# The second experts' transposed rows share the first layer's PSUM buffers

## Chip, cores and metric

The kernel runs on one core of a Trainium2 chip. The metric is the time of one execution on the device in microseconds (us). The engines of the core work side by side and wait for each other by semaphores: TensorE (PE in the rows; PEld is its weight load) multiplies matrices into PSUM, VectorE (DVE), ScalarE (ACT) and GpSimd (POOL) do the rest of the arithmetic, SyncE (SP) and GpSimd start transfers (DMAs).

## What is computed

Three layers follow each other: an attention with a local window and block summaries, a mixture of experts in which every row picks its best expert, and a second mixture in which each of eight experts takes exactly 384 rows, in the order of the scores. The third is where the change lies:

```python
def _moe2_ref(x, w_gate, w1, w2):
    N, D = x.shape            # 3072, 512
    E = w_gate.shape[1]       # 8
    cap = N // E              # 384
    logits = x @ w_gate
    order = np.argsort(-logits.flatten())
    ...                       # each row to its best expert that still has room
    for e in range(E):
        mask = assigned == e
        h = np.maximum(x[mask] @ w1[e], 0.0)      # 384 x 1024
        out[mask] = h @ w2[e]                     # 384 x 512
    return out
```

## The kernel before

The program runs in phases: attention (from the start to about 300 us), the first experts, and `phase_d`, the second experts, from about 340 us on. In `phase_d` three kinds of work are woven together on the engines. What is woven is fixed when the program is built: a small scheduler at the end of `phase_d` keeps estimated clocks (`now`, `dve`, `pool`) and decides in which order the pieces are written; at run time each engine goes through its own list in order and waits on semaphores.

The experts. One expert at a time has its 384 rows multiplied. Its first layer, `L1`, makes eight sums `dh_ps` (128 columns of the hidden layer each), each of 12 products (lines 961, 962, 963: high rows by high weights, low rows by high weights, high rows by low weights; four depth blocks). ScalarE (line 966) and VectorE (line 968) read each sum. Its second layer, `L2`, makes three sums `dz_ps` of 24 products (lines 975, 976, 977). A step counter `npc` runs over the 32 steps of the first layer and the 24 of the second.

The rows of the next expert. GpSimd gathers them (line 939, three gathers of 128 rows, tile `xg`) once the list of rows is ready; TensorE transposes each gather's 128 rows in four blocks into PSUM (line 950, `xT`); ScalarE copies them out as the high part `dxh` and VectorE subtracts to make the low part `dxl` (both on line 953). The scheduler puts the three groups of transposes (groups 0, 1 and 2 below) into the second layer of the expert before, at steps 34, 38 and 42 or later (`xts_step`). For expert 0, which has no expert before it, they come ahead of everything.

The selection. Which rows go to which expert is found by counting against thresholds, for one expert after the other, ahead of the experts' own work: in each of five steps VectorE builds a mask `p_g` (line 793), TensorE counts with it (line 806, tile `rt_ps`), and VectorE works out the next threshold from the counts (lines 809 to 826). At the end a list of row numbers is made, whose products (lines 895, 898) go through PSUM tile `dx_ps`.

Besides, the weights of the next expert are loaded in four chunks of a megabyte (line 522), and each is split into a high part by ScalarE (line 923) and a low part by GpSimd (line 932).

PSUM holds eight tiles in this phase: `st_ps` (state of the selection), `rt_ps`, `dx_ps`, three of `dh_ps` and two of `dz_ps`. A tile that is handed out again makes its first writer wait until the last reader of its former use is done. In the kernel before, the transposes of experts 1 to 7 take `dx_ps`, of which there is one; those of expert 0 (`cur is None`) take `dh_ps`.

Of the kernel before, what the change touches and what calls it, by code (L numbers as in the profile page):

```python
# [6 lines left out]
F32=mybir.dt.float32; BF=mybir.dt.bfloat16; F32R=mybir.dt.float32r; I32=mybir.dt.int32; U32=mybir.dt.uint32  # L7
AF=mybir.ActivationFunctionType; OP=mybir.AluOpType; AX=mybir.AxisListType
PSUM=bass.MemoryType.PSUM
B,H,S,D=4,8,768,64  # L10
# [898 lines left out]
def phase_d(nc,tc,ctx,I,st,out,R,W,wk,ps,cp):  # L909
# [4 lines left out]
    S={}  # L914
# [19 lines left out]
    def busy(x): dve[0]=max(dve[0],now[0])+x  # L934
# [11 lines left out]
            S[p]['raw']+=[load_chunk(W,w1,w2,e,j,G) for j in range(len(S[p]['raw']),4)]  # L946
    def xT(p,b):
        if b==0: S[p]['xh']=wk.tile([128,4,CAP],F32R,name="dxh",bufs=1); S[p]['xl']=wk.tile([128,4,CAP],F32R,name="dxl",bufs=1)
        q=(ps.tile([128,512],F32,name="dh_ps",bufs=3) if cur is None else ps.tile([128,512],F32,name="dx_ps",bufs=1)).rearrange("p (d c)->p d c",d=4); x=S[p]['x'][b]
        for d in range(4): T.transpose(q[:,d,:],x[:,128*d:128*d+128],ident)  # L950
        c=slice(128*b,128*b+128); h=S[p]['xh'][:,:,c]
        busy(0.65)
        A.copy(h,q); V.tensor_tensor(S[p]['xl'][:,:,c],q,h.bitcast(F32),op=OP.subtract)  # L953
# [51 lines left out]
    cur=None; curp=-1; npc=0  # L1005
# [38 lines left out]
    def xts_step():  # L1044
        q=curp+1
        if q<=7 and xts.get(q,3)<3 and now[0]>=gath_t[q]+4.5+1.0*xts[q] and (cur is None or npc>=34+4*xts[q]):
            xT(q,xts[q]); xts[q]+=1; now[0]+=0.45; return True
        return False
    hk=True; HOLD=3.0
    while True:  # L1050
# [13 lines left out]
        if cur is None:  # L1064
            q=curp+1
# [62 lines left out]
```

## Time and profile before

| | us |
|---|---|
| three runs | 712.67, 715.87, 718.59 |
| median of the runs | 715.87 |
| profiled execution | 713.7 |
| its span in the profile | 712.0 |
| TensorE busy in the span | 616.6 (87%) |
| VectorE busy | 506.4 (71%) |
| GpSimd busy | 359.2 (50%) |

In the rows of the timeline stand the start in us from the span's start, the duration in us, the engine, the line of the kernel, the operation, what it writes and reads (`out<-in`, buffer numbers left out), the shape, and how many instructions are merged. A bracket at the end gives the time for which the engine sat idle before, and what ended it. Products follow each other closer than their durations, since they are pipelined: the distance of two starts is what one costs.

### The profile page before, as it was taken

How to read it: one execution, taken by the hardware profiler on the slowest of the kernel's cores; microseconds unless marked ns; L12 is line 12 of the kernel's file. 1: busy time of each engine (PE TensorE's matmuls, PEld its weight loads, DVE VectorE, ACT ScalarE, POOL GpSimd, SP SyncE). 2: the span in 40 equal slices, each digit the busy share in tenths (PEclk: the TensorE clock that was granted, in tenths of full speed). 3: DMA queues.
4: the chain of work that ended last, by engine and by line, in shares of the span. 5: the costliest groups of instructions: out<-in, count | busy, mean ns of one | idle time of the engine just before them, and what ended most of it. 6: DMA issues, size and time to landing. Idle time of an engine off the chain costs nothing.

```text
span 712.0 us, 12786 instructions
## 1 busy us (share of the span) xinstructions
PE 616.6 (87%) x4427; PEld 503.1 (71%) x4427; DVE 506.4 (71%) x1896; ACT 314.5 (44%) x672; POOL 359.2 (50%) x388
## 2 busy tenths in 40 slices
PE   7787897888889998986379989799897998989997
PEld 4576686776577776763258768697785977869895
DVE  5666986999887899965766768588686886862120
ACT  5666775766327666610033142342423424245520
POOL 4333422436442736630056384773747737479751
PEclk9999998999799999996589999899998999999999
DMA  9899999958229866500160543605436064365201
GB/s 235 222 247 238 242 253 211 271 136 300 90 82 380 269 206 209 187 15 8 60 223 1 172 154 119 193 16 188 138 119 193 16 189 137 119 223 208 90 14 44
DMA packets 59778, 114.22 MB, mean 160 GB/s; under 512 B 13537, under 2 KB 23521, under 8 KB 58944
## 3 DMA queue, kind: packets, MB, share of 16 engines
q1 hardware_dynamic: 49968, 79.37, 38.9%
q0 software_dynamic: 9744, 34.02, 14.6%
q8 instruction: 35, 0.57, 0.3%
q14 instruction: 31, 0.25, 0.1%
HBM read 96.54 MB, written 14.88 MB: 156 GB/s over the span
## 4 chain that ended last, share of the span: by engine, by line
PE 33%; DVE 8%; issue 7%; POOL 3%; ACT 1%; DMA 1%; POOLq 0%; DVEq 0%
PE dh_ps L961 6%; PE dh_ps L962 5%; PE dh_ps L963 5%; PE dz_ps L975 4%; PE dz_ps L976 4%; PE dz_ps L977 4%; POOL wl L932 2%; DVE p_g L793 1%; PE rt_ps L806 1%; DVE dxl L953 1%; PE dx_ps L950 1%; PE dx_ps L895 1%; DMA xg<-xrows,p_ix 1%; POOL out_dram L982 1%; ACT dxh L953 1%
## 5 line engine op out<-in xcount | busy, mean ns | idle before, releaser
L932 POOL TENSOR_TENSOR wl<-wraw,wh 128x512 fp32r<-128x512 f32 x124 | 155.1, 1290 | 9.0 <-ACT wh L923 8.7
L961 PE MATMUL dh_ps<-dxh,wh 128*128 128x384 f32 x256 | 89.9, 351 | 0.7 <-ACT dxh L953 0.7
L923 ACT CAST wh<-wraw 128x512 fp32r<-128x512 f32 x128 | 73.6, 619 | 33.5 <-DMA wraw<-in_w1b_dram 33.4
L962 PE MATMUL dh_ps<-dxl,wh 128*128 128x384 f32 x256 | 86.8, 339 | 0.0
L963 PE MATMUL dh_ps<-dxh,wl 128*128 128x384 f32 x256 | 86.6, 338 | 0.0
L118 POOL TENSOR_TENSOR wraw<-wraw 96x512 f32<-96x512 f32 (+4 forms) x39 | 39.4, 1011 | 84.7 <-DMA wraw<-in_v_dram 82.2
L975 PE MATMUL dz_ps<-wh,dhh 128*128 128x512 f32 x192 | 82.1, 428 | 0.0
L977 PE MATMUL dz_ps<-wh,dhl 128*128 128x512 f32 x192 | 79.0, 411 | 0.0
L976 PE MATMUL dz_ps<-wl,dhh 128*128 128x512 f32 x192 | 79.0, 411 | 0.0
L982 POOL DMA_INDIRECT out_dram<-dz,io x24 | 24.5, 1021 | 104.2 <-ACT dz L980 102.4
L968 DVE SCALAR_TENSOR_TENSOR dhl<-dh_ps,dhh 128x384 fp32r<-128x384 f32 x64 | 35.1, 555 | 50.2 <-ACT dhh L966 49.9
L966 ACT ACTIVATE dhh<-dh_ps 128x384 fp32r<-128x384 f32 x64 | 31.5, 492 | 75.0 <-PE dh_ps L963 75.0
L980 ACT COPY dz<-dz_ps 128x512 f32<-128x512 f32 x24 | 14.1, 587 | 110.6 <-PE dz_ps L977 57.9
L505 POOL TENSOR_TENSOR wl<-wraw,wh 128x512 fp32r<-128x512 f32 (+1 forms) x26 | 48.9, 1904 | 26.0 <-ACT wh L504 22.0
L138 ACT ACTIVATE p_e<-s_sb,nm 128x118 f32<-128x118 f32 x192 | 59.7, 385 | 1.5 <-DVE nm L132 1.5
L961 PEld LDWEIGHTS dh_ps<-dxh,wh 128*128 128x128 f32 x256 | 48.9, 191 | 1.5 <-ACT dxh L953 0.9
L939 POOL DMA_INDIRECT xg<-xrows,p_ix x24 | 23.3, 971 | 51.7 <-DVE rrow L871 32.1
L962 PEld LDWEIGHTS dh_ps<-dxl,wh 128*128 128x128 f32 x256 | 48.6, 190 | 0.7 <-DVE dxl L953 0.4
L963 PEld LDWEIGHTS dh_ps<-dxh,wl 128*128 128x128 f32 x256 | 48.5, 190 | 0.0
L128 PE MATMUL s_ps<-kt,Q 128*128 128x118 f32 x192 | 41.5, 300 | 7.0 <-DVE kt L108 5.5
L504 ACT CAST wh<-wraw 128x1024 fp32r<-128x1024 f32 (+1 forms) x48 | 44.2, 983 | 6.1 <-DMA wraw<-in_w1a_dram 5.9
L132 DVE CUSTOM_DVE_ANT_0 s_sb<-s_ps,cst 128x118 f32<-128x118 f32 x192 | 42.0, 275 | 6.5 <-PE s_ps L128 2.7
(363 smaller groups left out, 1474.5 us busy)
## 6 DMA issues: line engine op xcount, KB each, us to landing
wraw<-in_w1b_dram SPq DMA_DIRECT2D x15, 1024.0 KB
wraw<-in_w2b_dram POOLq DMA_DIRECT2D x14, 1024.0 KB, 7.5
wraw<-in_w2a_dram SPq DMA_DIRECT2D x12, 1024.0 KB
wraw<-in_w1a_dram SPq DMA_DIRECT2D x10, 1024.0 KB
VV<-in_v_dram SPq DMA_DIRECT2D x16, 585.0 KB
kt<-in_k_dram SPq DMA_DIRECT2D x16, 412.0 KB
qd<-in_q_dram SPq DMA_DIRECT2D x16, 384.0 KB
wraw<-in_v_dram SPq DMA_DIRECT2D x8, 768.0 KB
```

Of the source, the lines that this page charges most:

```text
L132: V.tensor_tensor_reduce(out=sb[:,j,:],in0=p[:,j,0:118],in1=mk,scale=-0.125,scalar=3e38,op0=OP.add,op1=OP.min,accum_out=nm[:,j:j+1])
L138: A.activation(pe[:,j,:],sb[:,j,:],AF.Exp,bias=nm[:,j:j+1],scale=-1.0)
L504: (hi.tensor_copy if hi else nc.scalar.copy)(h[:,c],t[:,c])
L505: (lo or nc.vector).tensor_tensor(l[:,c],t[:,c],h[:,c].bitcast(F32),op=OP.subtract)
L923: A.copy(h[:,c],t[:,c])
L932: eng.tensor_tensor(l[:,c],t[:,c],h[:,c].bitcast(F32),op=OP.subtract)
L961: T.matmul(q,wh[:,c],s['xh'][:,d,:],start=(d==0),stop=False)
L962: T.matmul(q,wh[:,c],s['xl'][:,d,:],start=False,stop=False)
L963: T.matmul(q,wl[:,c],s['xh'][:,d,:],start=False,stop=(d==3))
L975: T.matmul(q,s['hh'][:,f,c0],wh[:,c],start=(f==0),stop=False)
L976: T.matmul(q,s['hh'][:,f,c0],wl[:,c],start=False,stop=False)
L977: T.matmul(q,s['hl'][:,f,c0],wh[:,c],start=False,stop=(f==7))
```

## The change

The transposes of every expert now take a tile of `dh_ps`, of which there are three, as those of expert 0 did. The tile `dx_ps` stays for the products of the lists.

```diff
     def xT(p,b):
         if b==0: S[p]['xh']=wk.tile([128,4,CAP],F32R,name="dxh",bufs=1); S[p]['xl']=wk.tile([128,4,CAP],F32R,name="dxl",bufs=1)
-        q=(ps.tile([128,512],F32,name="dh_ps",bufs=3) if cur is None else ps.tile([128,512],F32,name="dx_ps",bufs=1)).rearrange("p (d c)->p d c",d=4); x=S[p]['x'][b]
+        q=ps.tile([128,512],F32,name="dh_ps",bufs=3).rearrange("p (d c)->p d c",d=4); x=S[p]['x'][b]
         for d in range(4): T.transpose(q[:,d,:],x[:,128*d:128*d+128],ident)
```

No instruction changes its place on any engine; tiles and waits do. On TensorE, in the second layer of an expert in the middle, behind the counting products of line 806, groups 1 and 2 of the next expert's transposes (the names carry buffer numbers; DMASW stands for a gather's landing, DVE for VectorE):

```order
 L806 LDWEIGHTS p_g_6589
 L806 MATMUL rt_ps_6625<-p_oh_6494,p_g_6589 128x32
-L950 MATMUL dx_ps_6656<-cb_462,xg_6534 128x128 [waits DMASW0_49,DVE_49]
-L950 MATMUL dx_ps_6656<-cb_462,xg_6534 128x128 x3
-L950 MATMUL dx_ps_6666<-cb_462,xg_6536 128x128 [waits DMASW1_49,DVE_49]
-L950 MATMUL dx_ps_6666<-cb_462,xg_6536 128x128 x3
+L950 MATMUL dh_ps_6656<-cb_462,xg_6534 128x128 [waits DMASW0_49]
+L950 MATMUL dh_ps_6656<-cb_462,xg_6534 128x128 x3
+L950 MATMUL dh_ps_6666<-cb_462,xg_6536 128x128 [waits DMASW1_49]
+L950 MATMUL dh_ps_6666<-cb_462,xg_6536 128x128 x3
 L975 MATMUL dz_ps_6609<-wh_6217,dhh_6208 128x512
 L976 MATMUL dz_ps_6609<-wl_6218,dhh_6208 128x512
```

The rows stand where they stood; both groups lose the wait for VectorE and keep the one for their gather. On TensorE a little later, the next counting products, which come 12 products of the second layer behind group 2:

```order
-L806 LDWEIGHTS p_g_6652
-L806 MATMUL rt_ps_6690<-p_oh_6494,p_g_6652 128x32
+L806 LDWEIGHTS p_g_6652 [waits DVE_49]
+L806 MATMUL rt_ps_6690<-p_oh_6494,p_g_6652 128x32 [waits PE_49]
 L806 LDWEIGHTS p_g_6652
 L806 MATMUL rt_ps_6690<-p_oh_6494,p_g_6652 128x32
```

The wait for the mask, which the waits of the transposes included before, is now the counting's own; in the same way the second sum of the first layer (line 961) names a wait for TensorE's own earlier work. On VectorE, at the same place, the two masks and the readings of the three groups:

```order
 L793 TENSOR_TENSOR p_g<-st_ps,p_thr 128x768 [waits DVE_49]
-L953 TENSOR_TENSOR dxl<-dx_ps,dxh 128x4x128 [waits Activation_49] x2
+L953 TENSOR_TENSOR dxl<-dh_ps,dxh 128x4x128 [waits Activation_49] x2
 L809 TENSOR_TENSOR p_d<-rrow,rt_ps 32x8 [waits PE_49]
 L809 TENSOR_TENSOR p_d<-p_d,rt_ps 32x8 [waits DVE_49] x2
```

Here too nothing moved: the readings of groups 1 and 2 stand behind the second mask and ahead of the next step of the selection, as before.

## Rows read from the trace of the kernel before

**Rows 1.** Waits of TensorE, 340 to 712 us: line <- releaser: us, times, longest.

```profile
PE dx_ps L950 <- DVE dxl L953: 19.7, 11, 3.5
```

**Rows 2.** Timeline of TensorE around the transposes for expert 3.

```profile
495.84 0.60 PE L950 MATMUL dx_ps<-cb,xg 128*128 128x128 f32 x4
...
497.84 0.66 PE L950 MATMUL dx_ps<-cb,xg 128*128 128x128 f32 x4 [0.35 <-DVE dxl L953]
501.98 0.66 PE L950 MATMUL dx_ps<-cb,xg 128*128 128x128 f32 x4 [3.48 <-DVE dxl L953]
502.39 0.48 PE L975 MATMUL dz_ps<-wh,dhh 128*128 128x512 f32 x1
...
506.82 0.52 PE L806 MATMUL rt_ps<-p_oh,p_g 128*128 128x32 bf16 x6
```

**Rows 3.** Timeline of VectorE at the same place.

```profile
500.37 0.96 DVE L793 TENSOR_TENSOR p_g<-st_ps,p_thr 128x768 bf16<-128x768 f32 x1
501.24 0.68 DVE L953 TENSOR_TENSOR dxl<-dx_ps,dxh 128x512 fp32r<-128x512 f32 x1
...
507.37 0.17 DVE L809 TENSOR_TENSOR p_d<-rrow,rt_ps 32x8 f32<-32x8 f32 x1 [3.39 <-PE rt_ps L806]
...
512.38 0.17 DVE L809 TENSOR_TENSOR p_d<-rrow,rt_ps 32x8 f32<-32x8 f32 x1 [0.34 <-PE rt_ps L806]
```

**Rows 4.** Timeline of TensorE at the other five places, experts 1, 2, 4, 5, 6.

```profile
410.45 0.66 PE L950 MATMUL dx_ps<-cb,xg 128*128 128x128 f32 x4 [0.91 <-DVE dxl L953]
414.20 1.11 PE L950 MATMUL dx_ps<-cb,xg 128*128 128x128 f32 x4 [2.39 <-DVE dxl L953]
417.70 0.57 PE L806 MATMUL rt_ps<-p_oh,p_g 128*64 128x16 bf16 x12
...
457.23 1.11 PE L950 MATMUL dx_ps<-cb,xg 128*128 128x128 f32 x4 [3.48 <-DVE dxl L953]
462.66 0.52 PE L806 MATMUL rt_ps<-p_oh,p_g 128*128 128x32 bf16 x6
...
546.17 1.12 PE L950 MATMUL dx_ps<-cb,xg 128*128 128x128 f32 x4 [3.48 <-DVE dxl L953]
551.50 0.51 PE L806 MATMUL rt_ps<-p_oh,p_g 128*128 128x32 bf16 x6
...
590.79 0.66 PE L950 MATMUL dx_ps<-cb,xg 128*128 128x128 f32 x4 [3.48 <-DVE dxl L953]
595.63 0.52 PE L806 MATMUL rt_ps<-p_oh,p_g 128*128 128x32 bf16 x6
...
633.34 0.66 PE L950 MATMUL dx_ps<-cb,xg 128*128 128x128 f32 x4 [0.70 <-DVE dxl L953]
```

**Rows 5.** Stretch with busy times, granted clock (PEclk); a product at full clock.

```profile
505.00:506.00 1.00, 1.00 (x4) 0.72 (x4) 0.00 (x0) 0.00 (x0) 1.00 (x2) 0.50 0.29 107
...
527.94 0.40 PE L975 MATMUL dz_ps<-wh,dhh 128*128 128x512 f32 x1
```

**Rows 6.** Gathers: expert 0's second and third, the third's landing, expert 3's third.

```profile
358.56 0.97 POOL L939 DMA_INDIRECT xg<-xrows,p_ix  x1 [0.30 <-issue]
362.12 0.66 PE L950 MATMUL dh_ps<-cb,xg 128*128 128x128 f32 x4 [0.88 <-DMA xg<-xrows,p_ix]
...
359.83 5.16 DMA xg<-xrows,p_ix
...
494.44 0.96 POOL L939 DMA_INDIRECT xg<-xrows,p_ix  x1 [0.30 <-issue]
```

**Rows 7.** Timeline of GpSimd behind the second layer, and the next second layer's first product.

```profile
509.75 1.01 POOL L982 DMA_INDIRECT out_dram<-dz,io  x1 [3.36 <-ACT dz L980]
510.76 12.54 POOL L932 TENSOR_TENSOR wl<-wraw,wh 128x512 fp32r<-128x512 f32 x10
...
526.55 0.39 PE L975 MATMUL dz_ps<-wh,dhh 128*128 128x512 f32 x1
```

**Rows 8.** Stretch with busy times of PE, PEld, DVE, ACT, POOL, then PEclk.

```profile
650.00:660.00 10.00, 10.00 (x57) 9.11 (x55) 2.42 (x5) 3.08 (x6) 9.00 (x9) 1.00 0.37 134
```

## The prediction

> **What bounds the kernel now.** I read the page first: TensorE is busy for most of the span and carries a third of the chain that ended last, mostly by the matrix products of the second experts (lines 961 to 963 and 975 to 977). I then asked who waited for whom on TensorE from 340 us to the end. One wait stands out: the transposes of line 950 wait for VectorE's low halves of line 953, 19.7 us in 11 waits [rows 1].
>
> The timeline of one place shows what it is [rows 2]. While expert 2 is in its second layer, the rows of expert 3 are transposed in three groups. Group 0 starts at 495.84 without a wait, group 1 at 497.84 after 0.35 us, group 2 at 501.98 after 3.48 us. All three write the one buffer `dx_ps`, so each waits until VectorE has read the one before. VectorE's rows say why the second wait is long [rows 3]: its reading of group 1 (501.24, 0.68 us) stands behind a mask of the selection, `p_g` of line 793 (500.37, 0.96 us). That mask is the end of a chain of small steps, and the scheduler put it ahead of the reading. TensorE does not need the reading until the next expert begins.
>
> The other places read alike [rows 4]: 0.91 and 2.39 us before 410.45 and 414.20, 3.48 before 457.23, 546.17 and 590.79, 0.70 before 633.34. The remaining waits, one ahead of each of the last four, make up the rest of the 19.7. The transposes for expert 7 do not wait. That makes six places.
>
> A second loss hangs on the first. [...] The rows show 4.84 (501.98 to 506.82), 5.43, 5.33 and 4.84 [rows 2, 4]: 1.65, 2.24, 2.14 and 1.65 too much. At the first place six products follow: 0.41 + 1.39 = 1.80 against 3.50, so 1.70. Together 9.4 us.
>
> **The change.** It adds and removes no instruction, and no engine's order changes; only the buffer of 21 groups of transposes does, and with it the waits. Piece by piece:
>
> *Removed waits.* Three buffers take groups 0, 1 and 2, so no group waits for another. They held the first layer's sums 5, 6 and 7 before. What is read from those feeds the second layer's first block, which takes 24 products, 5.6 us, from 526.55, so they are free by about 532; group 0 comes at 495.84 + 44.19 = 540.0 (group 2 recurs after 546.17 - 501.98 = 44.19). Worth 19.7 us, and the 9.4 of slow clock if the clock then stays up: a ceiling of 29.1.
>
> *A new floor: the mask.* The next products of line 806 still need `p_g`. It ends at 500.37 + 0.96 = 501.33, so they can move from 506.82 to about 501.38, by 5.44 us [rows 2, 3]. What TensorE would gain there by itself is 0.35 + 3.48 + 1.65 = 5.48: the two happen to meet, and next to nothing is lost. Where the mask ends as far ahead of group 2 (0.65 us), the other middle places have room for 6.0, 5.9 and 5.4, again what TensorE would gain. At the first place there are only six products as cover: room for 417.70 - (414.20 - 0.60) = 4.10 against 0.91 + 2.39 + 1.70 = 5.00. The first layer follows at once there and needs both readings. Two of 0.68, the first begun 0.09 before the mask's end, end 1.3 us after the mask; TensorE comes to need them some 0.8 us after it (an estimate: the counting and one product), and waits 0.5. So it moves by 3.6, and loses 1.4.
>
> *VectorE behind it.* Its two readings now run back to back behind the mask, to about 502.6, and its next step (507.37, after 3.39 us of idling [rows 3]) can start there, 4.8 us earlier, where TensorE is 5.4 earlier: 0.65 short. One step later it idled 0.34 for TensorE (512.38), which takes up half; the rest would cost 0.3 x 4 = 1.2 us, if no other pause takes it. I count nothing, with 1.2 as the bound.
>
> *A new floor: the gather.* Group 2's rows must have landed. Their gather is issued at 494.44, and TensorE now wants them at 497.84 - 0.35 + 0.41 = 497.9. No row times this landing, so I bound it by expert 0's gathers, on which TensorE did wait: 358.56 to 362.12 is 3.5 us, the next took 5.16 [rows 6]. At 3.5 nothing is lost. At 5.2 the six places lose 1.4 (the mask's, as before), 0.9, 1.5, 1.5, 1.5 and 1.4, 8.2 us in all. The slow one is the last of its three, as here; but it ran at the start of the phase, where the first weights were still on their way beside it. I take the middle, 4.3 us, group 2 at 498.74: 0.6 lost at each of four places, none at the second. New waits are then 1.4 + 4 x 0.6 = 3.8.
>
> *What hides the rest.* GpSimd makes the low weights. Its ten after the scatter (510.76, 12.54 us) end 3.2 us before the second layer at 526.55 [rows 7]. TensorE comes 5.4 earlier, but the scatter had idled 3.36 for it and now starts at once, so the ten end at about 520.0 and the second layer starts at 521.1; its first product needs just the first of the last eight. Were that cover gone, each us would go to TensorE. Near the end, in 650 to 660, TensorE is busy 10.00 of 10 us [rows 8], so what comes in earlier goes out earlier. The new wait at the first layer's second sum is for TensorE's own work, already past: nothing.
>
> **Sum.** 19.7 + 9.4 - 3.8 = 25.3 us. The profiled execution took 713.7 (span 712.0), so 688.4; the median of the runs shown, 715.87, lies 2.2 above it and would give 690.6. I forecast 689.5, between the two. The unknown costs alone run from 713.7 - 27.7 = 686 (gathers land in 3.5) to 713.7 - 20.9 + 1.2 = 694 (in 5.2, and VectorE's rest).
>
> **Rivals.** *The clock falls all the same.* If the late gather leaves 1.5 us in front of group 2, or the eight transposes themselves let the clock drop, the 9.4 us are not saved (1.4 of them lay under the mask anyway): 713.7 - 20.9 + 8.0 = 701. For it: waits of 0.91 and 2.39 us were enough at the first place. Against it: single groups among products ran at clock 1.00 in 650 to 660 [rows 8]. [...]
>
> *The wait only moves.* If the buffers were still held, or VectorE set the pace, the saved time would come back at the next step: 714. Against it: VectorE idled 3.39 us at this very place, and the buffers are free 8 us early. For it: the mask's floor leaves no spare, so any lateness of the selection shows in full.
>
> *Slower.* The first layer's first three sums now take buffers that VectorE's readings must leave first. Were those late, TensorE would stall in the first layer, and the clock would fall there. The readings end at about 502.6; the first layer starts behind line 806 (501.4) and the six products that follow it (1.39 us), so at 502.8 at the earliest. For a loss of 1% (7.2 us) on top of the 25.3 saved the readings would have to end some 6 us later at each of five places. What keeps them early is the order on VectorE, where nothing stands between mask and readings, and the first layer needs what they write anyway. Time 722.
>
> **Chances.** Forecast (685 to 694): 0.66. Clock falls or gathers late (694 to 703): 0.22. The wait only moves: 0.08. Slower: 0.04. 1% is about what a measurement of this kernel can tell from no change, so faster by over 1% is 0.66 + 0.22 = 0.88, within 1% 0.08, slower 0.04. The range is 684 to 702.
>
> **What would show it.** Line 950 no longer waits for VectorE; what it still waits for is the gather, below 2 us. No stretch of clock 0.50 behind group 2. The distance from one expert's group 2 to the next falls from 44.2 to about 39 us. Products of line 806 start right behind their mask. If instead line 950 or 806 waits over 2 us in each expert, the floors were set too low; if clock 0.50 stays, the first rival holds; if the distance stays over 42 with VectorE never idle, the second; if lines 961 to 963 wait for VectorE, the third.

## The result

The changed kernel took 685.75 us (median of four runs, 682.42 to 691.74) beside 714.88 us for the kernel before (four runs, 712.67 to 718.59): a ratio of 0.960, with a 95% interval of 0.951 to 0.968. Faster, inside the range of 684 to 702 and 3.75 us below the 689.5 that were forecast. The profiled execution of the changed kernel took 682.42 us, its span 680.8.

Not all of the 31.2 us between the two profiled spans belong to the change. In the trace of the changed kernel expert 1's group 0 starts at 404.38, before at 408.45, and the diff touches nothing that runs ahead of that place. All comparisons below therefore go by **the stretch**: from the start of expert 1's group 0 to the end of the span. It holds all six places that the prediction speaks of.

| kernel | span | start of expert 1's group 0 | stretch |
|---|---|---|---|
| before | 712.0 | 408.45 | 303.6 |
| changed | 680.8 | 404.38 | 276.4 |
| changed, profiled a second time | 685.5 | 409.12 | 276.4 |

The second profile of the changed kernel agrees in the stretch and not in the start. So the change is worth 27.2 us here (predicted: 25.3), and the other 4.1 us between the first two traces lie in the stages before.

What TensorE waited for in the changed kernel, 330 to 681 us (line <- releaser: us in total, times, longest); the left-out lines are waits of the selection and its list, and two short ones ahead of expert 1:

```profile
PE dh_ps L950 <- DMA xg<-xrows,p_ix: 2.4, 5, 1.2
...
PE rt_ps L806 <- DVE p_g L793: 1.0, 3, 0.5
...
PE dh_ps L962 <- DVE dxl L953: 0.5, 2, 0.3
```

The 19.7 us of [rows 1] are gone: no line says that line 950 waits for VectorE. What line 950 still waits for is the gather, 2.4 us in all, and the 1.2 us among them is expert 0's, ahead of the six places.

The place of [rows 2], the transposes for expert 3, in the timeline of TensorE:

```profile
482.06 0.60 PE L950 MATMUL dh_ps<-cb,xg 128*128 128x128 f32 x4
...
483.53 0.62 PE L950 MATMUL dh_ps<-cb,xg 128*128 128x128 f32 x4
484.60 0.66 PE L950 MATMUL dh_ps<-cb,xg 128*128 128x128 f32 x4 [0.45 <-DMA xg<-xrows,p_ix]
485.01 0.48 PE L975 MATMUL dz_ps<-wh,dhh 128*128 128x512 f32 x1
...
487.90 0.52 PE L806 MATMUL rt_ps<-p_oh,p_g 128*128 128x32 bf16 x6
```

From group 0 to these counting products of line 806 it was 495.84 to 506.82, 10.98 us; it is now 482.06 to 487.90, 5.84 us. From this expert's group 2 to the next one's (at 523.49) it is 38.89 us, where it was 44.19. VectorE at the same place, to be read beside [rows 3]:

```profile
486.59 0.96 DVE L793 TENSOR_TENSOR p_g<-st_ps,p_thr 128x768 bf16<-128x768 f32 x1
487.47 1.28 DVE L953 TENSOR_TENSOR dxl<-dh_ps,dxh 128x512 fp32r<-128x512 f32 x2
488.78 0.17 DVE L809 TENSOR_TENSOR p_d<-rrow,rt_ps 32x8 f32<-32x8 f32 x1
...
493.46 0.17 DVE L809 TENSOR_TENSOR p_d<-rrow,rt_ps 32x8 f32<-32x8 f32 x1 [0.34 <-PE rt_ps L806]
```

The order on VectorE is the one before: the mask, then the readings. But the two readings (x2) now stand behind the mask together, and TensorE is not held by them. The next step of the selection (488.78) starts without the 3.39 us of idling.

The clock around group 2 in windows of TensorE (busy us of PE, PEld, DVE, ACT, POOL, then the granted clock):

```profile
444.00:450.00 6.00, 5.81 (x39) 4.50 (x38) 5.21 (x18) 4.23 (x8) 5.80 (x5) 1.00 0.94 295
...
484.00:490.00 6.00, 5.55 (x32) 4.39 (x31) 5.42 (x25) 3.29 (x7) 5.98 (x6) 1.00 0.93 295
...
400.00:680.80 280.80, 272.67 (x1538) 235.06 (x1536) 185.14 (x711) 110.72 (x212) 196.46 (x198) 1.00 0.42 139
```

It stays at 1.00 at the places, and its mean from 400 us to the end is 1.00; [rows 5] had 0.50 there. Over 400 to 712 us the mean before was 0.96.

### The profile page after: what moved, and what is told of

Same layout as the page of the kernel before. It is cut to its first block, busy times and chain, and to the rows that moved or that the text cites. A ratio compares the mean times of both kernels' runs of the same rounds, so it can differ in the third digit from the quotient of the medians.

```text
span 680.8 us, 12765 instructions
## 1 busy us (share of the span) xinstructions
PE 604.4 (89%) x4424; PEld 494.0 (73%) x4427; DVE 508.0 (75%) x1896; ACT 314.2 (46%) x672; POOL 359.0 (53%) x388
## 4 chain that ended last, share of the span: by engine, by line
PE 18%; issue 11%; POOL 11%; DVE 6%; DMA 3%; ACT 1%; POOLq 1%; DVEq 0%
POOL wl L932 9%; PE dh_ps L961 3%; PE dh_ps L962 3%; PE dh_ps L963 3%; DMA xg<-xrows,p_ix 2%; PE dz_ps L975 2%; PE dz_ps L976 2%; PE dz_ps L977 2%; POOL out_dram L982 2%; DMA wraw<-in_w1b_dram 1%; DVE p_g L793 1%; PE rt_ps L806 1%; PE dx_ps L895 1%; PE dh_ps L950 1%; ACT wh L923 1%
## 5 line engine op out<-in xcount | busy, mean ns | idle before, releaser
L975 PE MATMUL dz_ps<-wh,dhh 128*128 128x512 f32 x192 | 79.0, 411 | 0.0
L977 PE MATMUL dz_ps<-wh,dhl 128*128 128x512 f32 x192 | 76.0, 396 | 0.0
L976 PE MATMUL dz_ps<-wl,dhh 128*128 128x512 f32 x192 | 75.9, 395 | 0.0
```

Of the source, the lines that this page charges most:

```text
L975: T.matmul(q,s['hh'][:,f,c0],wh[:,c],start=(f==0),stop=False)
L976: T.matmul(q,s['hh'][:,f,c0],wl[:,c],start=False,stop=False)
L977: T.matmul(q,s['hl'][:,f,c0],wh[:,c],start=False,stop=(f==7))
```

## Experiments

Each is compared by the stretch, beside the changed kernel's 276.4 and the 303.6 of before. An added line shifts the numbers behind it by one: in the rows of e4, e6 and e7 line 950 reads as 951 and line 953 as 954, and in those of e4 to e7 line 962 reads as 963.

### One tile moved at a time

My theory was that two separate chains make the wait (group 1 behind group 0's reading, group 2 behind group 1's), and that the long one falls away when group 2 need not stand behind the reading that VectorE does after the mask. Three kernels give `dh_ps` to one group only: the line of e1 is shown against the kernel before, e2 has `b==2` in the same place and e3 `b==0`; `...` stands for the rest of the line, which stays.

```diff
-        q=(ps.tile([128,512],F32,name="dh_ps",bufs=3) if cur is None else ps.tile([128,512],F32,name="dx_ps",bufs=1))...
+        q=(ps.tile([128,512],F32,name="dh_ps",bufs=3) if cur is None or b==1 else ps.tile([128,512],F32,name="dx_ps",bufs=1))...
```

> Only group 1 of the transposes takes a buffer of the first layer's sums; groups 0 and 2 share dx_ps. Measured by the stretch from expert 1's group 0 to the end of the span: 303.5 us in the kernel before, 276.4 in the changed one. Theory (what costs is that a group follows right behind another in the same buffer): group 2 waits for VectorE's reading of group 0, which ends (497.78 at the place of rows 2) before TensorE wants the buffer (497.9), so the stretch is 276 to 277 and the time about 686. Rival (three buffers are needed, one for each group): group 2 waits again, 1 us or more at each of six places, and the stretch is 282 or more.

Measured: stretch 277.6, 687.15 us against 713.39 (ratio 0.964, interval 0.958 to 0.970).

> Only group 2 takes a buffer of the first layer's sums; groups 0 and 1 share dx_ps. Theory (the wait of group 2, behind the mask, is the one that costs): the waits of group 1 stay, 0.35 at four places, 0.91 and 0.70 at two, and are partly taken up by the gather and the mask; stretch from expert 1's group 0 to the end 277 to 279, time about 687, no stretch of clock 0.50. Rival (all three waits count alike): a third of the gain is missing, stretch 285.

Measured: stretch 277.1, 687.78 us (0.963, 0.957 to 0.968).

> Only group 0 takes a buffer of the first layer's sums; groups 1 and 2 share dx_ps, so group 2 still waits for the reading of group 1 behind the mask. Theory (that wait and the clock behind it are the whole price): next to no gain, about 0.7 at the last of the six places, stretch 302 to 303.5, time 713 to 716, clock 0.50 behind group 2 as before. Rival (one more buffer of any kind loosens the queue): a third to a half of the gain, stretch 290 to 295.

Measured: stretch 304.7, 713.2 us (0.999, 0.996 to 1.002).

TensorE at expert 3's place in e1:

```profile
487.64 0.62 PE L950 MATMUL dh_ps<-cb,xg 128*128 128x128 f32 x4
488.74 0.63 PE L950 MATMUL dx_ps<-cb,xg 128*128 128x128 f32 x4 [0.47 <-DVE p_d L809]
```

in e2:

```profile
489.49 0.66 PE L950 MATMUL dx_ps<-cb,xg 128*128 128x128 f32 x4 [0.34 <-DVE dxl L953]
489.98 0.63 PE L950 MATMUL dh_ps<-cb,xg 128*128 128x128 f32 x4
```

and in e3:

```profile
501.01 0.62 PE L950 MATMUL dx_ps<-cb,xg 128*128 128x128 f32 x4
505.68 0.66 PE L950 MATMUL dx_ps<-cb,xg 128*128 128x128 f32 x4 [4.04 <-DVE dxl L953]
```

In e3 the wait of group 1 is gone, and group 2 waits 4.04 us instead of 3.48: the 0.35 came back in it, and more. All its waits of line 950 on VectorE add up to what they were:

```profile
PE dx_ps L950 <- DVE dxl L953: 19.8, 6, 4.0
```

The 0.47 us left in e1 are like the 0.45 of the changed kernel at this place, where the gather ended them. That it is the gather here too is read from its issue: TensorE starts 3.96 us behind it (484.78 to 488.74), in the changed kernel 3.93. The row's own releaser is a small step of VectorE that has nothing to do with the tile. So it is the one step from group 1's tile to group 2's that costs, and either end of it may move. With two buffers in place of three, e1 and e2 keep all but 0.7 to 1.2 us of the gain. e1 lands 0.6 above the top of what was expected; at expert 2 TensorE waited 0.93 us for the gather, and not at all in the changed kernel. e3 lands 1.2 above: at its first place TensorE waited 3.37 us, the clock was 0.50 behind it from 416 to 420 us, and the place took 44.79 us to the next group 0 where it took 42.64 before.

### The clock apart from the wait

e4 is the kernel before, with products that nobody reads put ahead of group 2 at the four middle places. They keep TensorE busy while it would wait, and leave the wait as it is. `warm` makes 14 such products; the row below has 13 of them.

```diff
+        if b==2 and 2<=p<=5: warm(nc,st,R.psum(),14)
         q=(... name="dx_ps",bufs=1))...
```

> The kernel before, all groups in dx_ps; ahead of group 2 of experts 2 to 5 TensorE does 14 products of 512 columns that nobody reads, some 3.0 us, while it would wait for VectorE. The waits are as long as before, but TensorE is not idle in them. Theory (the clock falls because TensorE stands still, and its fall is a loss of its own): no clock 0.50 behind group 2, 1.65 to 2.24 us saved at each of the four places, 7.7 in all, stretch 295 to 297, time about 707. Rival (the clock falls for another reason, or the transposes let it fall): no saving or a loss, stretch 303 to 306.

Measured: stretch 296.5, 705.2 us against 713.39 (0.990, 0.985 to 0.995). TensorE at expert 3's place in e4:

```profile
491.67 3.19 PE L489 MATMUL rt_ps<-it,ones_b 128*128 128x512 bf16 x13
495.03 0.66 PE L951 MATMUL dx_ps<-cb,xg 128*128 128x128 f32 x4 [0.17 <-DVE dxl L954]
...
498.33 0.52 PE L806 MATMUL rt_ps<-p_oh,p_g 128*128 128x32 bf16 x6
```

Group 2 still starts 4.14 us behind group 1 (490.89), as before (497.84 to 501.98). But from group 2 to line 806 it takes 3.30 us and not 4.84. The four places gave 2.12, 1.54, 2.03 and 1.53 us, 7.2 together, and the stretch is 7.1 shorter. The slow clock is a cost of its own, and at these places standing still is what brought it about. The untreated first place is the control in the same trace. Windows behind group 2, there (410 to 412, behind a wait of 2.38 us) and at expert 3's place; the third number from the end is the granted clock:

```profile
410.00:412.00 2.00, 2.00 (x7) 1.62 (x6) 0.69 (x1) 1.10 (x2) 0.92 (x2) 0.50 0.92 358
...
495.00:498.00 3.00, 2.97 (x15) 2.52 (x16) 0.69 (x1) 2.15 (x4) 2.83 (x3) 1.00 0.92 352
```

### VectorE's slack

The prediction took VectorE's lateness of 0.65 us at nothing. e5 is the changed kernel, with one more reading (0.69 us) at each middle place.

```diff
     A.copy(h,q); V.tensor_tensor(S[p]['xl'][:,:,c],q,h.bitcast(F32),op=OP.subtract)
+    if b==2 and 2<=p<=5: V.tensor_tensor(S[p]['xl'][:,:,c],q,h.bitcast(F32),op=OP.subtract)
```

> The changed kernel, in which VectorE subtracts the low halves of group 2 a second time (0.63 to 0.69 us), right behind the first, at the middle four places (experts 2 to 5). Measured by the stretch from the start of expert 1's group 0 to the end of the span, which took 276.4 us in the changed kernel. If VectorE has slack there (my theory: its mask ended 0.5 to 0.6 us ahead of the next counting products, and it idled 0.34 one step later), 276.4 to 277.2, some 686 us in all. If VectorE sets the pace behind the readings (the rival 'the wait only moves'), 4 x 0.65 = 2.6 more: 279.0.

Measured: stretch 279.5, 3.1 longer; 689.27 us where the changed kernel beside it took 684.01. My theory missed. Not all of the 3.1 is VectorE's, though: at the first place, ahead of the edit, the clock fell, and 1.4 us were lost there against the second profile of the changed kernel (from group 0 to the next expert's 40.52 us and 39.14). TensorE there, and the window behind:

```profile
413.24 0.57 PE L806 MATMUL rt_ps<-p_oh,p_g 128*64 128x16 bf16 x12 [0.94 <-DVE p_g L793]
...
414.44 0.44 PE L963 MATMUL dh_ps<-dxl,wh 128*128 128x384 f32 x1 [0.26 <-DVE dxl L953]
```

```profile
416.00:418.00 2.00, 2.00 (x8) 2.00 (x7) 1.46 (x3) 0.52 (x2) 1.98 (x2) 0.50 0.76 305
```

The remaining 1.7 us arise behind the edited places. New waits of the next line 806, 0.33, 0.32 and 0.33 at experts 2, 4 and 5, are 1.0 of them; the rest lies in smaller steps. The first:

```profile
459.63 0.52 PE L806 MATMUL rt_ps<-p_oh,p_g 128*128 128x32 bf16 x6 [0.33 <-DVE p_g L793]
```

So 0.69 us more on VectorE cost some 0.43 us a place (1.7 over four): by this estimate about 0.25 us of slack was left. VectorE follows close behind TensorE here, which the rival "the wait only moves" had said in kind.

### How late the gather may be

The first rival asked what a late gather does. In e6 and e7 GpSimd does four or eight additions of a tile with itself ahead of group 2's gather, at the middle places of the changed kernel. One took 0.29 us, and one behind another 0.36. Without them the third gather comes 1.28 us behind the second. In e6 it came 2.81 behind (480.68 to 483.49), 1.5 us late where I had reckoned 1.0; in e7 the eight took 2.9, and it came 4.28 behind (487.25 to 491.53), 3.0 us late and not 2.0.

```diff
             t=st['xgp'].tile([128,ROW],F32,name="xg")
+            for _ in range(4 if b==2 and 2<=p<=5 else 0): G.tensor_tensor(lag,lag,lag,op=OP.add)   # e7: 8
             G.indirect_dma_start(out=t,...)
```

> The changed kernel with four small additions on GpSimd (128x64, an estimate of 0.25 us each from the 1.25 us of 128x512) ahead of the gather for group 2 at the middle four places, so that its rows land about 1.0 us later and TensorE waits 1.2 to 1.5 us in front of group 2. Stretch from the start of expert 1's group 0 to the end: 276.4 in the changed kernel. If each us of lateness costs one us and the clock holds: 276.4 + 4 x 1.0 = 280.4, granted clock 1.00 behind group 2. If a wait of this length lets the clock fall, as the first rival has it: 4 x 1.65 more, 287, and rows of clock 0.50.

Measured: stretch 280.1, 688.76 us. TensorE at expert 3's place, and the window behind:

```profile
484.84 0.62 PE L951 MATMUL dh_ps<-cb,xg 128*128 128x128 f32 x4
486.97 0.66 PE L951 MATMUL dh_ps<-cb,xg 128*128 128x128 f32 x4 [1.50 <-DMA xg<-xrows,p_ix]
```

```profile
489.00:491.00 2.00, 2.00 (x15) 1.50 (x14) 1.21 (x3) 0.81 (x2) 2.00 (x3) 1.00 0.96 309
```

The waits grew to 0.43, 1.50, 1.40 and 1.42 us, 4.1 us more than in the second profile of the changed kernel, and the stretch by 3.7. At experts 3, 4 and 5, where TensorE waited for the gather already, 1.5 us of lateness made 1.1 to 1.3 of wait; at expert 2 it made 0.43. Each us of wait cost about one (3.7 for 4.1), and the clock held at 1.00: the rival's condition was met, and its price did not come.

> The same with eight additions, about 2.0 us: TensorE waits 2.2 to 2.5 us in front of group 2. The clock fell behind a wait of 2.39 us in the kernel before, so I expect it to fall here: 276.4 + 4 x 2.0 + 4 x 1.65 = 291.0 us of stretch, clock 0.50 for some us behind group 2 at each place. If the clock holds, 284.4.

Measured: stretch 292.9, 702.96 us. At three of the four places the clock fell, at one it did not. TensorE's group 2 at two of them, and the windows behind:

```profile
453.44 0.66 PE L951 MATMUL dh_ps<-cb,xg 128*128 128x128 f32 x4 [1.90 <-DMA xg<-xrows,p_ix]
...
494.99 1.11 PE L951 MATMUL dh_ps<-cb,xg 128*128 128x128 f32 x4 [2.94 <-DMA xg<-xrows,p_ix]
```

```profile
453.00:457.00 4.00, 3.56 (x21) 2.83 (x22) 2.98 (x7) 2.15 (x4) 3.81 (x4) 1.00 0.94 271
497.00:499.00 2.00, 2.00 (x6) 1.51 (x6) 0.45 (x1) 1.28 (x3) 2.00 (x3) 0.50 1.06 317
```

The 16.5 us more than the changed kernel come apart as 9.8 of longer waits (1.90, 2.94, 2.78 and 2.84, less the 0.69 of the second profile), 5.4 of slow products behind the last three (from group 2 to line 806 5.94, 4.55 and 4.84 instead of 3.30), and 1.6 at the first place, near the 1.4 of e5, with no longer waits than there (0.9 and 0.3); the 0.2 that expert 2's line 806 waited for its mask fell away.

### The changed kernel again

> The changed kernel once more, beside the three. The stretch from the start of expert 1's group 0 to the end took 276.4 us; if the 4.06 us that it led before its first changed instruction are spread between runs and not of the change, the stretch stays within 0.5 us of that while the start of expert 1's group 0 (404.38) moves by some us.

Measured: stretch 276.4, start of expert 1's group 0 at 409.12; 684.01 us against 714.97 (0.957, 0.952 to 0.962). The lead of 4.06 us was spread: here the same kernel starts the stretch later than the kernel before did. Over all these traces that start lies between 403.6 (e4) and 410.6 (e3), whatever the kernel does behind it. The medians differ by 31.0 us here and by 29.1 above, 2 to 4 more than the stretch; executions of one kernel lie up to 9.3 us apart (682.42 to 691.74), and whether any of this belongs to the change these runs do not show.

## Why the prediction held, step by step

**Removed waits, 19.7.** Right in kind, about 1.0 too low. Line 950 no longer waits for VectorE, and e1, e2 and e3 show which step of it cost. Two things were not in the 19.7. At expert 2 the wait of group 1 is put down to "issue" and not to VectorE:

```profile
453.09 0.66 PE L950 MATMUL dx_ps<-cb,xg 128*128 128x128 f32 x4 [0.34 <-issue]
```

And group 1 starts 1.47 to 1.49 us behind group 0 at the four middle places, where it was 2.00 to 2.01 (495.84 to 497.84 in [rows 2], 482.06 to 483.53 now). That is 0.52 less, for a wait that the rows give as 0.34 or 0.35: some 0.7 more in four places.

**The slow clock, 9.4.** Right in kind, 0.7 too high. Behind the wait of 3.48 us the granted clock was 0.50 [rows 5], and the sum counted what a middle place took above 3.19 us: 0.41 of transposes (501.98 to 502.39 [rows 2]) and twelve products at 0.232, as six took 1.39 in an undisturbed row (526.55 to 527.94 [rows 5, 7], where the clock was 1.00). In the changed kernel the transposes and twelve products take 3.30 us at clock 1.00 (484.60 to 487.90), 0.11 more at each of four places. At the first place it is 2.05 (407.01 to 409.52, less a wait of 0.46) where the sum had 1.80. e4 gave back 7.2 at the four middle places where the working had 7.7.

**The mask's floor, 1.4 at the first place.** Right in place, the waits too high in this trace: TensorE waited there 0.46 for the mask and 0.26 for the low halves of the reading.

```profile
407.01 0.66 PE L950 MATMUL dh_ps<-cb,xg 128*128 128x128 f32 x4 [0.23 <-DMA xg<-xrows,p_ix]
...
409.52 0.56 PE L806 MATMUL rt_ps<-p_oh,p_g 128*64 128x16 bf16 x12 [0.46 <-DVE p_g L793]
...
410.72 0.44 PE L962 MATMUL dh_ps<-dxl,wh 128*128 128x384 f32 x1 [0.26 <-DVE dxl L953]
```

With the 0.23 of waiting for the gather that makes 0.95. In the second profile, where group 2's gather had landed in time, the two waits are 0.94 and 0.26, nearer the 1.4. The place as a whole came out as reckoned: from group 0 to the next expert's it took 42.64 us before and 38.95 now, 3.7 less, where the working has 3.6.

**The gather's floor, 2.4.** This term was sized too high. Its place and order were right: group 2 came to need its rows 2.09 us behind group 0 (2.06 by the working). But a gather took 3.9 us from issue to the transposes and not 4.3: GpSimd issued expert 3's at 480.67, and TensorE began at 484.60.

```profile
480.67 0.96 POOL L939 DMA_INDIRECT xg<-xrows,p_ix  x1 [0.30 <-issue]
```

At experts 4 and 5 the waits were 0.27 and 0.29, at experts 2 and 6 none. All waits for gathers at the six places add up to 1.2 us. The middle between the two bounds, 3.5 and 5.2, was a guess; the quicker end was nearer.

**The sum.** New waits came to 2.15 us (1.24 for gathers, 0.72 at the first place, 0.19 at expert 2's line 806) and not 3.8, 1.65 more gain. With the 0.34 and the 0.7 of group 1 that the removed waits lacked, and 0.7 less from the clock, 25.3 becomes 27.3, beside the 27.2 measured. So the forecast was close in part because its errors had both signs. From the profiled 713.7 the stretch alone gives 686.5; of the 3.75 us between the median and the forecast, 1.9 are the larger gain; the rest lies ahead of the stretch or in the spread of executions.

**VectorE's 0.65, taken at nothing.** Nothing was lost, but the reason was thin. VectorE was late by 0.33 only (its step began 0.88 us behind line 806 at 487.90, where it had begun 0.55 behind at 507.37), because TensorE itself came 0.45 late from the gather: two shortages at the same place were paid once. What took up the 0.33 was not the pause named in the prediction: the 0.34 for TensorE one step later is there undiminished. It was the pause ahead of it, in which VectorE waits for ScalarE (line 966), before and now:

```profile
511.48 0.56 DVE L968 SCALAR_TENSOR_TENSOR dhl<-dh_ps,dhh 128x384 fp32r<-128x384 f32 x1 [0.60 <-ACT dhh L966]
...
492.56 0.56 DVE L968 SCALAR_TENSOR_TENSOR dhl<-dh_ps,dhh 128x384 fp32r<-128x384 f32 x1 [0.28 <-ACT dhh L966]
```

At experts 2, 4 and 5 that pause, 0.54 to 0.55 before, is gone altogether, and there e5 made TensorE wait. So the term was nothing by a pause that the working had not looked at.

**GpSimd and the end of the kernel.** The low weights of line 932 are nowhere among TensorE's waits above, so what was taken as hidden was hidden. They do now make up 9% of the chain that ended last, and 7% in the second profile, where it was 2% before; TensorE waits for none of it:

```profile
POOL wl L932 9%; PE dh_ps L961 3%; PE dh_ps L962 3%; PE dh_ps L963 3%; DMA xg<-xrows,p_ix 2%; PE dz_ps L975 2%; PE dz_ps L976 2%; PE dz_ps L977 2%; POOL out_dram L982 2%; DMA wraw<-in_w1b_dram 1%; DVE p_g L793 1%; PE rt_ps L806 1%; PE dx_ps L895 1%; PE dh_ps L950 1%; ACT wh L923 1%
```

**The rivals.** *The clock falls all the same* did not come about in the changed kernel, and e6 met its condition (1.5 us in front of group 2) without its price. Nor did eight transposes with a pause between them let it drop: the 1.48 us from 483.53 to 485.01 in the changed kernel and the 2.54 us from 484.84 to 487.38 in e6 hold nothing else, and the clock was 1.00 behind both (484 to 490 and 487 to 491 us). So the case of 701 did not come. In one form the rival is real: at the first place the clock fell to 0.50 in e5 (416 to 418 us), for 1.4 us, and e7 took 1.6 more there. *The wait only moves* is what e3 shows. As for the whole change, the buffers were free, as forecast. *Slower*: line 962 waited 0.26 us for the readings at the six places; the stall in the first layer did not come.

## What to carry to other kernels

When a producer refills one buffer, look in the reader's queue for what stands between two reads. Here a mask that had nothing to do with the buffer stood there, TensorE waited 3.5 us at a time, and a second buffer at the right one of two steps gave nearly all of the gain (e1, e2), at the wrong one none (e3). Count a wait of TensorE together with the slow products behind it, which were a third of the gain here (8.7 of 27.2 us), and then ask what has the least slack once the wait is gone: the gather had none at experts 3 to 5, and VectorE about 0.25 us.

## What the runs showed of the chip

The clock held at 1.00 behind waits of 0.45 (changed kernel), 1.4 to 1.5 (e6) and 1.90 us (e7), and fell to 0.50 behind 2.38 us (e4), 2.8 to 2.9 (e7) and 3.48 (before). But the wait in front is not all: at the first place the same two pauses, 0.94 and 0.26 us, left the clock at 1.00 in the second profile of the changed kernel and brought it to 0.50 in 416 to 418 us in e5, at a cost of 1.4 us. With 0.9 for the first of them it held in e1 and e6, at 1.00 from 410 to 420 us, and e7 took 1.6 us more at that place. What tells these apart no run here shows.
